# A gated linear recurrence followed by an MLP mixer: one batch's v loaded in fp32, and some transposes moved to the DMA crossbar

## The chip, the cores and the metric

The kernel runs on one core of one Trainium2 chip. The core has five engines that work side by side, each through its own list of instructions in order: PE (TensorE, the matrix multiplier), DVE (VectorE), ACT (ScalarE), POOL (GpSimd) and SP (SyncE, which here only starts transfers). Sixteen DMA engines move data between memory and the chip's buffers; SP and POOL each feed them through a queue of their own. The metric is the device time of one execution in microseconds (us); lower is better. Before the change the median of three runs is 182.91 us (181.78 to 183.03).

## The reference

The input is `q`, `k`, `v` and `alpha`, each of shape (batch 4, heads 8, sequence 768, head size 48), and four weight matrices. All of it is fp32.

```python
for t in range(S):                               # S = 768, per batch and head
    state = alpha[t][:, None] * state + outer(k[t], v[t])   # 48 x 48
    y[t] = q[t] @ state
x  = y with the heads side by side               # (4, 768, 384)
h  = relu(x.T @ w_tok1) @ w_tok2                 # mixes along the sequence, 768 -> 256 -> 768
u  = x + h.T
out = u + relu(u @ w_ch1) @ w_ch2                # mixes along the channels, 384 -> 1536 -> 384
```

## The kernel before

**Attention in chunks.** The recurrence is computed in chunks of 128 steps, six per batch, numbered n = 0 to 23 over all batches (batch 3 is n = 18 to 23). In a chunk, ACT takes the logarithm of alpha (`ln`, line 412), PE sums it along the steps (`cum`, line 418), and ACT exponentiates it with both signs (`ea`, `ei`). POOL multiplies k (`kk`, line 434), and POOL or DVE multiplies q (`qq`, line 438), into bf16. PE then transposes both with eight 128x128 transposes into PSUM (`trk`, `trq`, line 454), and ACT or DVE copies the result to the buffer `tp` (line 458). From `tp` PE computes the 128x128 scores (`gt`, line 469), DVE masks them (`mask`, line 472), and PE multiplies them with v and adds the carried state (`y`, lines 507 and 511). `st`, `sa` and `ss` update the state. The result `x` is copied out of PSUM.

**Batch 0 in pairs.** Batch 0 is handled by `attention_pair`: two neighbouring chunks of four heads each, with rows taken two at a time, so that one run in memory is 384 bytes long (two rows of 48 fp32 numbers). Its alpha, k and q come through SP's queue in loads of four heads (`load_pair`, line 744). Its v comes through POOL's queue in six transfers that turn fp32 into bf16 on the way (`load_vz`, line 723) and write into the places between zeros of a buffer `vz`: rows 0 to 63 hold one chunk's v in the first half and zeros in the second, rows 64 to 127 the reverse. The zeros are set once (line 952). `st` and `y` (lines 634 and 666) read `vz`. All other loads (`load`, line 733) bring one chunk with all heads, in runs of 192 bytes.

**Mixer.** Per batch, `mixer` does `tok1` (line 766), `ht` (relu), `tok2` (line 788), `u` (line 798, the sum x + h), then needs u with channels on the partitions. For the first half of batch 0 that is computed directly (`tt`, lines 812 and 817). For every other half PE transposes u in nine 128x128 transposes (`utp`, line 834), in parts of six and three, and DVE or ACT copies them to `ut` (line 840). Then follow `ch1` (line 853), `rt` (relu, lines 860 and 861), `ch2` (line 875), the last sum `o` (line 881) and the store `out` (line 884) on SP's queue. `wload` (line 400) brings the weights through POOL's queue, in eight transfers that also turn fp32 into bf16: `wt1`, `wt2`, three of `wc1` and three of `wc2`.

**The order.** All operations form a graph with dependencies and buffers. `schedule` is a list scheduler that runs when the program is built: with assumed durations it takes, of the operations that could start about now, the one with the lowest number in `RANKS` (a list of names; loads of batch 0 have their own list `LOADS`), and also chooses between engines and buffers. `NOT_BEFORE` gives a few operations an earliest planned time, and `SW` is a fixed list of the stretches in which POOL's transfers are assumed to slow SP's. The result is only an order: on the chip every engine works through its list and waits for its inputs, not for planned times. `fill` puts 70 multiplications without use (`warm_`, line 377) into the list for PE where nothing else is ready; 18 more (`warm`, line 366) start the program. The first fill begins after 5 us of planned time.

Of the kernel before, what the change touches and what calls it, by code (L numbers as in the profile page):

```python
# [9 lines left out]
BF16 = mybir.dt.bfloat16  # L10
AF = mybir.ActivationFunctionType
ALU = mybir.AluOpType
# [28 lines left out]
ch2_3_5b_1 trk6 vb18 utp2_0_0 out1_0 mask17 ss9 cum17 u1_4 ch1_1_1_11 rt3_1_10 ch2_2_5_1 ei14 ch2_2_4_2 tok2_2_3
gt13 out0_1 kk21 cum9 vb9 ch1_0_0_6 ut3_0_1 y10 u3_1 trq15 tok1_0_1_0 utp3_1_0 tok1_2_0_3 rt0_0_5 gt2 gt23 kk2 o0_3
tok1_1_0_3 rt0_1_8 ch2_3_3_1 ea6 tok1_1_1_0 rt1_1_8 trk12 ea17 rt2_0_8 ch1_3_0_4 trk19 ei11 lvz1 ch1_3_1_10 ut1_0_1
ut0_0_2 mask0 trk1 trq6 rt2_1_4 st9 ut2_0_0 gt6 st6 cum23 ea13 ch1_0_0_4 rt0_0_1 ut0_1_0 rt1_1_1 gt1 ch2_0_2_0
utp3_1_1 ch1_3_0_10 rt1_0_7 ch1_0_0_5 gt4 ch2_0_5_1 y17 ss14 ch1_2_0_5 rt2_1_3 trq20 u1_1 ch2_3_2_1 trq12 ea21
tok1_1_0_5 tok2_0_4 ea23 tk5 vb23 ch1_2_1_11 ch1_3_0_7 u3_0 u3_2 ch2_3_1_1 u0_2 ss12 ei8 kk3 st12 mask5 ht2_1 aq11
kk17 trk18 aq5 mask14 ln15 tp9 ht0_0 ch2_2_2_1 sa20 ln7 gt22 ch1_3_1_9 tok2_1_0 tok1_1_1_3 ln12 o2_2 rt3_0_11 tk0
ss1b ei9 st16 rt0_1_5 u2_5 u0_1 y2 o3_5b qq4 rt3_0_6 ch2_2_3_1 o2_1 ei18 trk4 aq0 trk21 ut0_0_1 ss2 tp7 ln19 ln5 y1
cum7 cum2 y0 gt16 ea4 tok1_0_1_5 y21 vb12 ln2 ea19 o3_4 ea8 rt1_0_5 ch1_3_0_6 ch1_0_0_0 ei5 ch1_2_0_10 st15 rt0_0_3
rt2_1_7 aq7 vb19 out3_0 rt3_0_2 ut1_1_1 sa7 ut3_1_0 rt3_1_5 out2_4 ei7 tok2_3_4 mask10 ei13 tt0_1 trk9 ei2 ln21  # L50
ch2_2_2_2 mask7 trq23 utp1_0_0 ch1_1_1_10 rt0_1_10 ei23 ea11 ch1_3_1_7 ch1_1_1_5 o3_3 lvz2 cum15 out3_2 rt1_1_10
ch1_0_1_7 sa22 st21 out1_5 trk8 ss7 ch2_3_2_0 ch1_0_0_1 kk6 qq5 tp18 x7 ss3 gt15 cum8 tp16 trq22 kk0 aq23 ss1 qq23
ln4 wwt1 u1_0 st18 st20 x10 utp0_1_0 qq14 ch2_1_2_0 ch1_3_0_0 out0_3 rt0_1_7 aq10 rt3_1_2 rt2_1_1 o3_5a trk23 ln18
x3 ut2_1_1 rt0_1_3 out3_3 trk20 gt0 st3 st7 rt3_1_9 st1 rt2_1_2 tp6 tok2_0_3 ch1_0_0_2 ut2_1_0 trk16 wwc20 rt1_1_4
ea10 rt3_0_9 ch1_0_0_3 st4 y9 tok2_0_5 rt1_1_11 wwc10 y16 trq3 ch1_0_0_11 utp0_1_1 rt3_0_1 ln1 ss6 ch1_3_1_6
ch1_3_1_2 ea3 ch1_0_0_9 rt0_1_0 trq19 trq8 ch1_1_1_0 tok1_3_0_0 u3_3 x17 aq15 tok2_0_2 qq10 x1 qq21 tok2_3_0 out3_1
ch2_1_0_2 lvz5 trq13 aq16 ch1_0_1_4 tok2_0_1 ch1_0_1_1 ch1_0_1_11 aq12 rt1_0_1 cum11 ch1_0_1_6 trq11 out1_4 tok2_3_1
tok1_3_0_3 ch1_0_0_7 ch1_2_0_7 ch1_0_1_3 o2_3 ut0_0_0 vb22 tok2_1_1 tok2_0_0 mask15 ea12 trq21 st14 u2_0 gt3
ch2_0_2_1 tok2_1_3 wwc21 ch1_0_1_5 aq3 u0_4 rt0_0_11 st22 ch1_0_1_0 vb16 trk7 tp23 wwc22 mask8 ss3b rt0_0_8 trq5
qq19 rt2_1_10 ch1_0_1_9 mask21 ss5 rt0_1_4 ei1 tok1_1_0_0 ln22 tok2_2_1 ch2_3_4_2 rt3_0_10 tk1 tok1_1_1_5 ln9 st19  # L60
out0_4 utp1_0_1 y7 ch1_0_1_10 rt0_0_6 ch2_3_5a_1 kk15 x15 kk8 rt3_0_4 ch1_0_1_8 ch2_0_0_0 aq18 utp2_0_1 rt1_0_11
out3_4 out1_1 ch2_2_4_0 ch2_3_0_0 y11 ch2_0_5_0 ea15 ch1_3_1_5 vb13 o0_4 tq3 u2_1 rt3_1_4 aq1 ch1_3_1_1 rt2_1_6
tok1_3_1_0 qq20 ch2_0_1_0 ss4 ch2_2_0_2 ch2_0_3_0 tok2_1_5 tp10 ss22 trq0 ch1_1_1_9 ch1_3_0_8 mask4 y23 u0_0
ch1_3_0_5 rt0_0_9 tok1_0_1_3 o1_2 vb21 mask6 rt0_1_9 tok1_0_0_5 ch1_2_1_2 rt2_1_0 tok2_1_4 rt3_0_8 st5 lvz0 mask3
utp3_0_1 rt1_0_9 cum22 aq8 kk13 ch2_2_1_1 ss21 ch2_3_1_0 rt1_0_2 trq10 out1_3 ln3 kk19 gt14 rt3_0_3 rt2_0_3 tok2_2_2
ch2_3_1_2 mask13 ch1_2_1_1 ut2_0_1 ch1_1_1_7 kk22 ch1_2_0_4 ln8 tq1 tok1_3_1_5 o2_4 aq17 o3_1 ch2_2_5_2 ht1_1 ei12
aq20 y22 ss15 y18 ln14 ch1_2_1_7 kk5 ch1_1_1_2 ss10 gt11 rt1_0_6 st3b ch1_2_0_2 ch2_1_3_2 st13 rt0_1_6 ss16
ch2_0_3_2 y12 rt1_1_2 out0_5 ch1_1_0_10 tq5 cum0 u2_2 tok1_2_0_5 vb20 out3_5b x22 tok2_2_0 rt2_1_5 ht1_0 ch2_3_0_1
vb6 out0_0 cum20 ch1_1_0_5 vb7 gt17 x4 rt3_1_0 ei4 rt2_0_5 o2_5 gt10 utp2_1_0 ch1_1_1_6 aq13 ei20 cum6 ch1_3_1_0
rt0_0_4 ch2_1_1_1 trk22 o0_0 ch2_3_4_1 ea7 wwc12 ch1_1_1_8 ch1_1_0_1 rt0_0_0 trk14 ei21 ln20 ch2_0_1_2 cum18 u1_2  # L70
ch1_2_1_8 ch1_2_0_3 ch1_1_0_2 ss19 ch2_1_1_0 rt2_0_7 rt3_1_6 out1_2 o3_0 out2_5 ch2_2_1_2 ch1_2_1_3 tok2_2_4 u2_3
ch1_3_0_3 qq0 tq0 rt0_1_1 cum19 rt1_0_0 ei17 ch2_3_5b_2 u0_3 x2 ln11 ch1_2_1_10 o0_5 x12 wwc11 trq18 ht3_1 rt0_0_10
qq9 rt2_0_11 ch2_3_2_2 ch1_1_0_0 vb14 ch1_1_0_3 o2_0 tok1_2_1_3 y5 st8 ei10 ss2b tp21 qq15 rt2_0_9 aq6 trk11 y15
ei22 tok1_2_1_5 aq14 ch1_2_0_8 rt0_0_2 utp2_1_1 sa14 ch2_1_2_2 trq14 ch1_3_1_3 ch1_1_0_9 x19 tok1_2_0_0 rt3_1_8 kk11
rt0_1_2 mask18 trk15 utp1_1_0 vb8 tp22 o0_1 kk1 u0_5 mask9 trk0 ch1_1_0_6 rt3_1_7 ch1_3_1_8 ch1_1_0_11 ch1_2_0_1
ch1_2_0_0 ch2_2_0_1 qq16 ss18 rt2_1_8 u3_5 ch1_3_0_1 out2_2 ut1_0_0 ea0 x13 cum14 sa21 aq2 ea9 rt0_0_7 ea5 st0
ch1_2_1_5 sa16 ch2_3_5a_2 ch2_1_5_2 st1b ch1_1_0_4 kk7 y19 out2_1 mask22 ch2_1_3_0 ln6 tp14 x14 st2b tok2_2_5 cum13
# [132 lines left out]
def schedule(ops, slots, sw=()):  # L210
# [20 lines left out]
    while ready:  # L231
# [41 lines left out]
        if o.dma:  # L273
            o.done = dmas.land(o.dma[0], t, *o.dma[1:])
# [779 lines left out]
```

## Time and profile before

| what | value |
|---|---|
| median of three runs | 182.91 us |
| the profiled execution's own time | 182.94 us |
| its span (first to last instruction) | 181.2 us |
| PE busy | 173.9 us, 96% of the span |
| ACT busy | 108.5 us, 60% |
| DVE busy | 105.4 us, 58% |
| POOL busy | 59.7 us, 33% |
| SP's queue, all loads and stores | 22.42 MB, 59.6% of 16 engines |
| POOL's queue, v of batch 0 and the weights | 3.74 MB, 14.2% of 16 engines |
| granted TensorE clock | 1.00 |

The profile is of one execution. The span leaves out 1.7 us of the execution's own time that lie around it. Busy times of PE overlap, since a multiplication begins before the one ahead of it has ended: one 128x384 multiplication is listed with 326 ns, but 36 in a row took 5.85 us. Idle time of an engine that is not the limit costs nothing. Shares over the whole span are averages over stages with different limits, and the stages are what has to be read.

### The profile page before, as it was taken

The numbers are of one execution on the slowest core, as the hardware profiler recorded it, in microseconds if no ns is written. First come the engines' busy times: TensorE is split into PE (matmuls) and PEld (weight loads), VectorE is DVE, ScalarE is ACT, GpSimd is POOL, SyncE is SP. The second block draws the span as 40 slices with busy tenths as digits, with TensorE's granted clock in tenths as the row PEclk, the third lists the DMA queues.
The fourth block names the chain that finished last, engine by engine and source line by source line (L and its number), as shares of the span: only waits on it lengthen the run. The fifth ranks groups of instructions, "written<-read, shape, count | busy, mean of one in ns | idle before, by whom it ended". The sixth has DMA issues, their size and how long they took to land.

```text
span 181.2 us, 4740 instructions
## 1 busy us (share of the span) xinstructions
PE 173.9 (96%) x1922; PEld 120.7 (67%) x1922; DVE 105.4 (58%) x190; ACT 108.5 (60%) x219; POOL 59.7 (33%) x94
## 2 busy tenths in 40 slices
PE   7897899999999999999899999999999999999994
PEld 4575788677676676677677666577666566676663
DVE  6674676694972665886975579565556652130142
ACT  3456785577894567799787675879732204948000
POOL 8922886020942336456361722403030000000000
PEclk9999999999999999999999999999999999999999
DMA  5999999998999899999999999910002121110123
GB/s 133 201 202 245 225 176 200 194 191 171 203 196 198 159 194 178 201 185 238 205 217 182 228 169 205 259 60 4 0 0 89 45 87 43 47 43 0 43 90 130
DMA packets 93861, 26.45 MB, mean 146 GB/s; under 512 B 88080, under 2 KB 93456, under 8 KB 93840
## 3 DMA queue, kind: packets, MB, share of 16 engines
q1 hardware_dynamic: 87984, 22.42, 59.6%
q0 software_dynamic: 5856, 3.74, 14.2%
q8 instruction: 15, 0.25, 0.6%
q14 instruction: 6, 0.05, 0.1%
HBM read 25.17 MB, written 4.72 MB: 165 GB/s over the span
## 4 chain that ended last, share of the span: by engine, by line
PE 64%; DMA 23%; SPq 4%; ACT 2%; DVE 2%; issue 1%; POOL 1%; DVEq 0%; POOLq 0%; ACTq 0%
PE ps L853 21%; PE ps L875 19%; DMA at_pair<-in_alpha_dram 15%; SPq L744 4%; PE ps L766 3%; PE ps L788 3%; DMA vt_pair<-in_v_dram 3%; PE ps L454 3%; DMA qt_pair<-in_q_dram 3%; DMA at<-in_alpha_dram 3%; PE ps L377 2%; PE p L469 2%; PE ps L834 1%; PE ps L507 1%; PE ps L666 1%
## 5 line engine op out<-in xcount | busy, mean ns | idle before, releaser
L853 PE MATMUL ps<-ut,wc 128*128 128x384 bf16 x288 | 54.3, 326 | 0.9 <-DVE ut L840 0.5
L875 PE MATMUL ps<-wc,rt 128*128 128x384 bf16 (+1 forms) x300 | 52.7, 319 | 0.0
L860 ACT ACTIVATE rt<-ps 128x384 bf16<-128x384 f32 x85 | 41.8, 494 | 12.9 <-PE ps L853 12.4
L853 PEld LDWEIGHTS <-wc 128*128 128x128 bf16 x288 | 30.7, 114 | 13.3 <-issue 1.7
L875 PEld LDWEIGHTS <-rt 128*128 128x128 bf16 x300 | 27.8, 98 | 15.5
L881 DVE TENSOR_TENSOR o<-ps,u 128x384 f32<-128x384 f32 (+1 forms) x25 | 13.3, 540 | 21.6 <-PE ps L875 21.2
L472 DVE TENSOR_TENSOR gtm<-p,u 128x1024 bf16<-128x1024 f32 x18 | 22.0, 1220 | 6.8 <-PE p L469 6.8
L434 POOL TENSOR_TENSOR pkk<-kt_pair,ia 128x384 bf16<-128x384 f32 x15 | 15.3, 1017 | 24.3 <-ACT ia L428 24.2
L798 DVE TENSOR_TENSOR u<-ps,x 128x384 bf16<-128x384 f32 x24 | 12.7, 550 | 6.7 <-PE ps L788 6.7
L458 ACT COPY tp<-ps 128x1024 bf16<-128x1024 bf16 x13 | 13.2, 1014 | 3.3 <-PE ps L454 3.3
L377 PE MATMUL ps<-warm_in 128*128 128x256 bf16 x70 | 13.9, 290 | 0.0
L445 POOL TENSOR_TENSOR acq<-a,bm 128x8 f32<-128x8 f32 x18 | 5.7, 317 | 24.0 <-ACT a L426 22.5
L412 ACT ACTIVATE la<-at_pair 128x384 bf16<-128x384 f32 x15 | 7.9, 528 | 8.7 <-DMA at_pair<-in_alpha_dram 8.6
L788 PE MATMUL ps<-ht,wt 128*128 128x384 bf16 x48 | 11.0, 326 | 0.0
L438 DVE TENSOR_TENSOR pkq<-qt_pair,a 128x384 bf16<-128x384 f32 x9 | 7.1, 784 | 6.1 <-DMA qt_pair<-in_q_dram 4.4
L492 DVE TENSOR_TENSOR sum<-ps,ss 128x384 f32<-128x384 f32 x12 | 6.6, 552 | 6.2 <-PE ps L483 6.2
L766 PE MATMUL ps<-x,wt 128*128 128x384 bf16 x48 | 9.9, 326 | 0.0
L428 ACT ACTIVATE ia<-ps 128x384 f32<-128x384 f32 x18 | 8.9, 492 | 1.3 <-PE ps L421 1.3
L840 ACT COPY ut<-ps 128x384 bf16<-128x384 bf16 (+1 forms) x7 | 4.2, 611 | 9.0 <-PE ps L834 9.0
L426 ACT ACTIVATE a<-ps 128x388 f32<-128x388 f32 x18 | 8.8, 491 | 0.6 <-PE ps L421 0.5
L515 ACT CAST x<-ps 128x384 bf16<-128x384 f32 x12 | 5.8, 481 | 5.1 <-PE ps L511 5.0
L611 DVE TENSOR_TENSOR gtm<-p,mask_pair 128x1024 bf16<-128x1024 f32 x6 | 7.3, 1223 | 2.0 <-PE p L606 1.8
(118 smaller groups left out, 267.1 us busy)
## 6 DMA issues: line engine op xcount, KB each, us to landing
out_dram<-o SPq DMA_DIRECT2D x23, 192.0 KB, 3.0
at_pair<-in_alpha_dram SPq DMA_DIRECT2D x21, 192.0 KB, 4.5
kt_pair<-in_k_dram SPq DMA_DIRECT2D x21, 192.0 KB, 4.7
qt_pair<-in_q_dram SPq DMA_DIRECT2D x21, 192.0 KB, 4.8
vt_pair<-in_v_dram SPq DMA_DIRECT2D x14, 192.0 KB, 4.4
wc<-in_moe_w_ch_dram POOLq DMA_DIRECT2D x6, 384.0 KB, 9.1
vt<-in_v_dram SPq DMA_DIRECT2D x4, 192.0 KB, 4.0
wt<-in_moe_w_tok_dram POOLq DMA_DIRECT2D x2, 384.0 KB, 7.1
```

Source lines behind the costliest of these rows:

```text
L377: last = g.op("PE", f"warm_{i}", lambda e, ps=ps: e.matmul(ps()[:, 0:256], lhsT=E.warm_in[:, 0:128], rhs=E.warm_in, start=True, stop=True, ...
L428: g.op("ACT", f"ei{n}", lambda e: e.activation(ia(), cum()[:, 0:HD], AF.Exp, scale=-1.0), act_us(384), reads=[cum], writes=[ia])
L434: g.op("POOL", f"kk{n}", lambda e: e.tensor_tensor(pkk()[:, :, 0:D], T["kt"](), hd(ia()), ALU.mult), (1.03, 1.0), reads=[T["kt"], ia], wri ...
L458: lambda e: (e.copy if e is E.act else e.tensor_copy)(tp(), ptp().bitcast(BF16).rearrange("p (j t) -> p j t", t=128)),
L472: g.op("DVE", f"mask{n}", lambda e: e.tensor_tensor(gtm(), E.p23.rearrange("p (j t) -> p j t", t=128), E.mask8, ALU.mult), (1.24, 1.22), r ...
L766: e.matmul(ps()[:, 0:HD], lhsT=E.b_wt1[:, kc, m * 128:m * 128 + 128], rhs=x[kc](), start=(kc == 0), stop=(kc == NS - 1), skip_group_check= ...
L788: e.matmul(ps()[:, 0:HD], lhsT=E.b_wt2[:, kc, i * 128:i * 128 + 128], rhs=ht[kc](), start=(kc == 0 and not summed), stop=(kc == NDT - 1))
L798: g.op("DVE", f"u{b}_{i}", lambda e, ps=ps, t=t, i=i: e.tensor_tensor(t(), ps()[:, 0:HD], x[i](), ALU.add), dve_us(384), reads=[ps, xt[i]] ...
L853: e.matmul(ps()[:, 0:384], lhsT=E.by_four[mc // 4][:, kc, mc % 4, :], rhs=uts[half]()[:, kc * 384:kc * 384 + 384], start=(kc == 0), stop=( ...
L860: e.activation(rtt[mc]()[:, cs], ps()[:, 0:384], AF.Relu) if e is E.act else
L875: e.matmul(ps()[:, 0:n], lhsT=rtt[mc]()[:, i * 128:i * 128 + 128], rhs=E.b_wc2[:, mc, cs], start=(mc == 0), stop=(mc == NDC - 1), skip_gro ...
L881: g.op("DVE", f"o{tag}", lambda e, ps=ps, t=t, i=i, cs=cs, n=n: e.tensor_tensor(t()[:, cs], ps()[:, 0:n], u[i]()[:, cs], ALU.add), dve_us( ...
```

## The change

1. **v of batch 0.** `load_vz` is gone. v is now loaded like q, in fp32 by SP's queue (`ldvt`), and 12 new operations `vc` cast it into the six buffers `b_vz` beside the zeros, 64 partitions by 384 elements each, on ACT, DVE or POOL.
2. **Loads of batch 0.** Only the first pair of chunks is still loaded in two groups of four heads. The other two pairs are loaded with all eight heads at once. There are 16 loads in place of 18 and six transfers on POOL's queue. The list `LOADS` begins with v.
3. **k with q of batch 3.** For n = 18 to 23 k and q are written into one buffer (`s_pk`), and one DMA on SP's queue, `dtk`, transposes it through the crossbar into `tp`. `trk`, `trq` and the copy `tp` are gone there.
4. **u of batches 2 and 3.** Three tiles of u share one buffer (`s_u3`), and one DMA on SP's queue per half, `dtu`, transposes it into `ut`. `utp` and the copies `ut` are gone there. `ch1` reads the new layout through `channels`.
5. **Buffers and planner.** `rt` has 18 buffers and, from batch 1 on, the six `vz` buffers too (before 24); `u` has 12 (13), `o` 6 (7), `pkk` 4 (6), `acq` 5 (6). In the planner SP waits when over 2048 runs are in flight, and a transpose holds SP until the transfers ahead of it are done. `RANKS`, `LOADS`, `NOT_BEFORE` and `SW` are new throughout.

```diff
-LOADS = {n: i - 2999.0 for i, n in enumerate("""ldat0 ldkt0 ldat2 ldqt0 ldkt2 ldat4 ldqt2 ldat1 ldqt1 ldat3 ldat5 ldqt4 ldkt1 ldkt3 ldqt3 ldkt4 ldkt5 ldqt5""".split())}
-NOT_BEFORE = {"lvz0": 3.0, "lvz1": 3.6432229280593225, "lvz2": 3.5646344861793087, "lvz3": 3.0, "lvz4": 3.0,
-              "lvz5": 6.784296118108255, "wwt1": 18.201532689715037, "wwt2": 20.604694224156404, "wwc10":
-              23.228101551750406, "wwc11": 33.44407754651961, "wwc12": 26.882706927650386, "wwc20":
+LOADS = {n: i - 2999.0 for i, n in enumerate("""ldvt0 ldat1 ldvt1 ldvt2 ldat0 ldkt0 ldkt1 ldat2 ldqt1 ldqt0 ldkt2 ldqt2 ldkt4 ldat4 ldqt4 ldvt4""".split())}
+NOT_BEFORE = {"wwt1": 15.268526730144032, "wwt2": 17.868047160368754, "wwc10": 37.09580914814636, "wwc11":
+              3.784711466738922, "wwc12": 28.05532928830701, "wwc20": 46.56128458051416, "wwc21":
...
+            if e == "SP":
+                turned = dmas.hw_end - o.dma[1] if o.dma[3] == 129 else 0.0
+                free[e] = max(free[e], dmas.gate(), turned)
...
+    SPLIT = (0,)
+    CROSS_KQ, CROSS_U = tuple(range(18, 24)), (2, 3)
...
+        if crossbar:
+            g.op("SP", f"dtk{n}", lambda e: e.dma_start_transpose(
+                tp(), tk().rearrange("p w h d -> p (w h d)")), (1.3, 1.3), reads=[tk], writes=[tp],
+                dma=("hw", 0.9, 1.0, 129))
+        else:
+            g.op("PE", f"trk{n}", lambda e: f_tr(e, 1, pkk), (0.225, 0.225 + DRAIN), reads=[tk], writes=[ptp])
+            g.op("PE", f"trq{n}", lambda e: f_tr(e, 0, pkq), (0.225, 0.225 + DRAIN), reads=[tq], writes=[ptp])
...
-        vz = T["vz"]
+        vz = g.tile(self.s_vz[ci])
+        for hh in range(2):
+            g.op(("ACT", "DVE", "POOL"), f"vc{n}_{hh}", lambda e, r=slice(64 * hh, 64 * hh + 64), hh=hh: (
+                e.copy if e is E.act else e.tensor_copy)(E.b_vz[ci][r, hh], of("vt")[r]),
+                [(0.39, 0.49), (0.36, 0.35), (0.53, 0.5)], reads=[T["vt"][grp]], writes=[vz], joint=True, lock=True)
...
-            g.op("POOL", f"lvz{n + hh}", lambda e, hh=hh, ts=ts: e.dma_start(
-                t()[64 * hh:64 * hh + 64, hh, :, :],
-                E.d_v[b, :, ts:ts + 128, :].rearrange("h (p c) d -> p h (c d)", c=2)),
-                (0.68, 0.68), writes=[t], joint=True, at=6.0 + 3.0 * ci + 0.1 * hh, dma=("sw", 1.6, 0.37))
...
+            if b in self.CROSS_U:
+                g.op("SP", f"dtu{b}_{half}", lambda e, t=t, h=ut3[3 * half]: e.dma_start_transpose(
+                    t().rearrange("p (j t) -> p j t", t=128), h()), (1.35, 1.35), reads=[ut3[3 * half]],
+                    writes=[t], dma=("hw", 1.0, 1.0, 129))
+                uts.append(t)
+                continue
...
+        def channels(t, kc):
+            if b in self.CROSS_U:
+                return t.rearrange("p (i j t) -> p j i t", i=3, j=3)[:, kc]
+            return t[:, kc * 384:kc * 384 + 384]
```

More of the change, by code (lines that the diff above doesn't have):

```diff
@@ L74 @@
[L74 to L77, printed above, removed]
-ln16 o1_5 o1_1 trq4 ei15 out3_5a y20 ch2_1_5_0 ch1_3_1_11 ch2_2_3_0 o0_2 ch1_1_0_8 ch2_2_4_1 mask20 ch2_2_5_0 aq4
@@ L206, in land @@
         self.hw_end = t + left
+        self.flying.append((t + left, runs))
         return t + left + 1.2
```

249 lines of the change are left out of this document (136 added, 113 removed), and 4 rows, old and new, of the table PLAN.

## The prediction

> **What bounds the kernel now.** I read the page first: the span, the busy engines, the slices, the chain.
>
> ```profile
> span 181.2 us, 4740 instructions
> PE 173.9 (96%) x1922; PEld 120.7 (67%) x1922; DVE 105.4 (58%) x190; ACT 108.5 (60%) x219; POOL 59.7 (33%) x94
> ...
> DMA  5999999998999899999999999910002121110123
> ...
> PE 64%; DMA 23%; SPq 4%; ACT 2%; DVE 2%; issue 1%; POOL 1%; DVEq 0%; POOLq 0%; ACTq 0%
> ```
>
> PE is busy nearly throughout. The DMA engines are as full up to slice 26 (about 118 us), and the chain gives them 23%. So the question is which of the two sets the end, and the stages answer it:
>
> ```profile
> 120.00:140.00 20.00, 20.00 (x238) 13.83 (x237) 11.48 (x17) 12.58 (x26) 3.01 (x4) 1.00 0.07 24
> 140.00:160.00 20.00, 20.00 (x146) 13.02 (x143) 7.88 (x15) 7.31 (x15) 0.00 (x0) 1.00 0.14 51
> ```
>
> ```profile
> 30.60:177.80 147.20, 146.08 (x1553) 99.61 (x1551) 84.76 (x134) 90.48 (x184) 38.95 (x57) 1.00 0.68 136
> ```
>
> The columns are the stretch, its length, the busy time of PE, PE's weight loads, DVE, ACT and POOL, then PE's clock, the DMA share and GB/s. From 30.6 to 177.8 us PE idles 147.20 - 146.08 = 1.1 us, at clock 1.00. A busy PE need not be one at its rate, so I look at the chain in order of time:
>
> ```profile
> 41.21 0.45 PE ps L454 x8
> ...
> 120.91 0.44 PE ps L834 x6
> ...
> 160.40 5.85 PE ps L853 x36
> 166.25 11.73 PE ps L875 x84
> ```
>
> 36 multiplications of 384 columns in 5.85 us are 0.1625 us each, packed without a gap. The 23% of DMA in the chain is how the walk back passes through loads in the middle; PE did not stop for them there. So **PE's work from 30.6 us on sets the end**: what leaves PE there comes off the time, and what delays the start of that stretch is added.
>
> What sets 30.6? The last logarithm of batch 0, and the first multiplications of the mixer:
>
> ```profile
> 17.20 0.52 ACT L533 ACTIVATE la<-at_pair 128x384 bf16<-128x384 f32 x1 [0.81 <-DMA at_pair<-in_alpha_dram]
> ```
>
> ```profile
> 30.59 1.14 PE L766 MATMUL ps<-x,wt 128*128 128x384 bf16 x6
> ```
>
> ```profile
> 17.00:30.60 13.60, 12.41 (x225) 10.27 (x223) 9.44 (x16) 9.75 (x19) 10.13 (x14) 1.00 1.09 203
> ```
>
> Batch 0's last alpha is there at 17.2 us, and 13.4 us of work on POOL (10.13 busy), ACT (9.75) and DVE (9.44) in turns follow. Up to 30.6 us PE partly does fill. The head is thus bound by batch 0's loads and then by that chain.
>
> **The change part by part.**
>
> *Transposes off PE.* Batch 3: six chunks of eight, 48. Batches 2 and 3: four halves of nine, 36.
>
> ```profile
> L454 PE MATMUL ps<-id,pkk 128*128 128x128 bf16 x72 | 7.0, 219 | 0.0
> L454 PE MATMUL ps<-id,pkq 128*128 128x128 bf16 x72 | 7.0, 219 | 0.0
> ...
> L834 PE MATMUL ps<-id,u 128*128 128x128 bf16 x63 | 5.7, 219 | 0.0
> ```
>
> The 219 ns overlap; in the chain eight take 0.45 us and six 0.44 us, or 0.056 us each (0.073 in the short piece, with its run-in). I take 0.056: 84 x 0.056 = **4.7 us** off PE. Batch 3's first transposes stand here:
>
> ```profile
> 100.57 0.39 PE L454 MATMUL ps<-id,pkk 128*128 128x128 bf16 x4
> ```
>
> So all of it comes off after 100 us, where PE is full. The copies out of PSUM go too (six `tp`, eight parts of `ut`):
>
> ```profile
> L458 ACT COPY tp<-ps 128x1024 bf16<-128x1024 bf16 x13 | 13.2, 1014 | 3.3 <-PE ps L454 3.3
> ```
>
> They lie on ACT and DVE beside a full PE (12.58 and 11.48 of 20 us), so they are worth nothing by themselves. The new access of `ch1` reads the same 384 columns in three pieces of 128, in 144 multiplications. At the rate of 128-column ones (3 x 0.056 = 0.169 against 0.1625 us) that would be 0.9 us, at best 0; I take 0, since it stays one instruction.
>
> *Crossbar transposes.* The trace has none, so I bound one by other transfers. SP's queue late in the kernel holds stores alone, and the landing times are min, median and max:
>
> ```profile
> 113.52 65.22 SPq L884 DMA_DIRECT2D out_dram<-o  x20
> ```
>
> ```profile
> DMA to landing us min/median/max: 1.6/1.9/5.1
> ```
>
> ```profile
> kt_pair<-in_k_dram SPq DMA_DIRECT2D x21, 192.0 KB, 4.7
> ```
>
> Low end 1.9 us (a quiet queue), high end 4.7 us (among loads). The path replaced is 0.45 + 1.01 = 1.5 us. So a result comes 0.4 to 3.2 us later than PE's, ten times. What hides that is PE's other work; today's order leaves this between transposes and scores:
>
> ```profile
> 128.60 0.39 PE L454 MATMUL ps<-id,pkq 128*128 128x128 bf16 x4
> 128.83 1.63 PE L853 MATMUL ps<-ut,wc 128*128 128x384 bf16 x9
> 130.38 0.42 PE L469 MATMUL p<-tp 48*64 48x128 bf16 x16
> ```
>
> That is 1.8 us filled with `ch1`. The new planner assumes 1.0 + 0.9 + 1.2 = 3.1 us from issue to landing, and its order will put about that much `ch1` and `ch2` in between; 120 to 160 us hold enough of it. The first ones, from 100.6 us on, meet a full DMA queue, those after 113.5 us a quiet one. I take 0.3 us lost in all; the bounds are 0 and, with no cover, 32 us. Behind a waiting `dtk` or `dtu` on SP stand later loads and stores. Loads run far ahead (the last issue is before 113.5 us, and the scores at 130.38 still work on what they brought), so a few us of lateness there cost nothing; a store costs only at the end, where no transpose is left.
>
> *v by SP's queue, in fp32.* POOL's six issues go, 3.65 us of five of them ahead of the first `kk`:
>
> ```profile
> 3.02 3.65 POOL L723 DMA_DIRECT2D vz<-in_v_dram  x5
> ```
>
> The bytes read stay. The packet counts of 2 to 6, 8 to 14 and 2 to 21 us:
>
> ```profile
> q1 hardware_dynamic: 2483, 0.93, 95.7%
> ```
>
> ```profile
> DMA packets 4372, 1.22 MB, mean 204 GB/s; under 512 B 4372, under 2 KB 4372, under 8 KB 4372
> ```
>
> ```profile
> q1 hardware_dynamic: 10201, 3.66, 85.3%
> q0 software_dynamic: 3168, 0.59, 36.7%
> ```
>
> SP's queue alone made 2483 / 4 = 621 packets per us; both queues together 4372 / 6 = 729. Batch 0 has four inputs of 768 x 384 fp32 in runs of 384 bytes, 3072 x 4 = 12288 packets. Today they are through at about 20 us (13369 by 21 us, the last of them batch 1's); by one queue from 2 us on, 12288 / 621 = 19.8 us bring it to 21.8: up to **1.8 us later**. The Trainium skill ("DMA: Bandwidth & Descriptors", Issuing engines are not separate DMA queues) says that transfers of all queues run on the same 16 engines and that spreading them only saves issue time; by that rule this term would be 0 and the head's upper bound lower by it. The rows, 621 against 729, speak against the rule here.
>
> *Weights in the head.* `wc11` may now start at 3.8 us of planned time, when POOL has nothing else, so it goes first on POOL. The size of such a transfer, and what one does to SP's queue, at 32 to 38 us and, without one, at 40 to 44:
>
> ```profile
> wc<-in_moe_w_ch_dram POOLq DMA_DIRECT2D x6, 384.0 KB, 9.1
> ```
>
> ```profile
> q0 software_dynamic: 929, 0.92, 90.2%
> q1 hardware_dynamic: 1178, 0.22, 30.6%
> ```
>
> ```profile
> q1 hardware_dynamic: 3451, 0.65, 83.5%
> ```
>
> SP's rate falls from 863 to 196 packets per us, by 77%, and 384 KB (0.39 MB) of weights at 0.92 / 6 = 0.153 MB per us last 2.6 us: 2.0 us of delay for the loads of the head. `wt1` starts earlier too and may meet the last loads.
>
> *Against that:* k of both chunks of a pair now arrives ahead of the next pair (today `kt1`, `kt3` and `kt5` come late), POOL is lighter by 3.65 x 6 / 5 = 4.4 us, and only v, needed last in a chunk, ends late. Alpha of the last pair ends at packet 10240 of 12288: 2 + 10240 / 621 = 18.5 us, 20.5 with `wc11`, where today it is 17.2. From there only the last two chunks remain.
>
> *Casts.* Twelve `vc` on half the partitions; the same free size costs
>
> ```profile
> L440 ACT CAST vb<-vt_pair 128x384 bf16<-128x384 f32 x6 | 3.1, 519 | 0.3 <-DMA vt_pair<-in_v_dram 0.2
> ```
>
> 0.52 us each, 6.2 us over three engines in 25 us, of which at most the last one (0.5) is on the path. The zeros are as many bytes as before; fewer buffers could stall, but each batch needs 12 `rt`, and 24 remain after batch 0. For the head I sum bounds: later data +3.8, casts +0.5, against the 3.65 us of issues that stand ahead of POOL's first `kk` today and may come off in full. I take **0**, near the middle of -3.65 to +4.3.
>
> *The refitted orders* touch every engine's list. With 1.1 us idle from 30.6 on there is next to nothing left to win; a bad order could lose, which I leave to the range.
>
> **Sum**, against the profiled execution's own 182.94 us (its span and 1.7 us around it; the median of the runs is 182.91): -4.7 + 0.3 + 0 = -4.4, **178.5 us**.
>
> **Rivals.**
>
> *The head gets shorter.* POOL's first `kk` no longer waits for 3.65 us of issues, and k comes in time. Against it: the two-queue rate. At -2.5 us: 176.0.
>
> *The head gets longer.* One queue and `wc11` cost the full 3.8 us and nothing is won back; PE's work is still 4.4 us less: 178.5 + 3.8 = 182.3, within 1%. For it: the rates above; against: 13.4 us pass today between the last alpha and 30.6, so data isn't all.
>
> *The crossbar is late, and the kernel slower.* Place: scores of chunks 18 to 23 and `ch1` of four halves. A transpose that waits for the transfers ahead and lands after 4.7 us plus 1.3 us of issue takes 6.0 where the order has 3.1: 2.9 us each where PE, which keeps its order, comes to the scores first. Two exposed ones (5.8 us) eat the gain; from three on (8.7) the kernel is slower by over 1%: 178.5 + 3 x 2.9 = 187.2. For it: the full queue before 113 us. Against: PE's slip at the first one gives the later ones room, and the later ones come after 113.5 us.
>
> *The crossbar works block by block.* Eight or nine blocks of 128x128 in turn, each with a small store's least landing time, 1.6 us, would hold SP's queue for 6 x 12.8 + 4 x 14.4 = 134 us; from 100.6 us on, with `ch1` and `ch2` of the last half (5.85 + 11.73 us) behind them, the end would be near 252. The Trainium skill ("VectorE: DVE Perf Modes", The three transpose paths) advises TensorE where PSUM will do, and gives 1309 ns for one 128x128 block by the crossbar against 390 on TensorE; estimated by that page, block by block, the queue would be held for 110 us. No run here shows it yet, and transfers of 192 KB landing in 1.9 us are a sign against such slow pieces.
>
> **How the numbers follow.** Forecast 0.46 (own range 177 to 181), shorter head 0.11, longer head 0.18, late crossbar 0.20, block by block 0.05. A measurement of this kernel tells some 1% from no change: faster means below 181.1, slower above 184.7. Faster 0.46 + 0.11 = 0.57; same 0.18; slower 0.25. For 8 in 10 the range leaves out the last case and most of the late crossbar: 175.8 to 186.0.
>
> **What would show it.** Right: no L454 rows for batch 3, L834 with 27 transposes in place of 63, PE idle after the head still some 1 to 2 us, the first mixer row (L766) within 3 us of 30.6. Wrong: PE waits on a DMA at the scores or at `ch1` after 95 us (crossbar), the first L766 past 34 us (head), or waits on SP's queue that reach PE. A transpose's issue and landing will be in the DMA rows.

## The result and the profile after

The changed kernel takes 185.14 us (median of four runs, 184.81 to 185.68) against 182.91 us before; the ratio, from runs on one chip, is 1.014 with an interval of 1.009 to 1.019. A second measurement of the same kernel, shown below, gave 1.010 (1.005 to 1.016). **It is slower, by about 1%.** The prediction said 178.5 us, faster, with 175.8 to 186.0 as its range. Ratios here and below leave out runs more than 1.5% above the fastest of the same kernel, which matters most for `e_u3`, where three of six are left out.

The page of the changed kernel, with the lines that answer to those quoted of before:

```profile
span 183.1 us, 4587 instructions
PE 169.2 (92%) x1838; PEld 117.6 (64%) x1838; DVE 98.3 (54%) x182; ACT 108.0 (59%) x227; POOL 57.4 (31%) x89
...
DMA  5999999999999998999999899999530053320113
...
PE 70%; DMA 16%; ACT 6%; SPq 4%; DVE 2%; issue 1%; POOL 1%; ACTq 0%
```

PE has the 84 multiplications less that the change takes away (1922 to 1838) and 4.7 us less busy time (173.9 to 169.2), as forecast. Its share of the span fell, though, from 96% to 92%: the work went and idle time came. DMA stays full longer, up to slice 28 in place of 26.

The idle time shows in the timeline of PE at the end of the head (first the kernel before, then the changed one), and in the stretch from there to PE's end (columns: stretch, length, busy time of PE, its weight loads, DVE, ACT, POOL, then clock, DMA share, GB/s):

```profile
31.79 1.14 PE L766 MATMUL ps<-x,wt 128*128 128x384 bf16 x6
```

```profile
34.62 1.38 PE L788 MATMUL ps<-x,wt 128*128 128x384 bf16 x6
```

```profile
34.60:179.40 144.80, 140.86 (x1466) 95.22 (x1465) 77.29 (x122) 87.47 (x186) 38.24 (x54) 1.00 0.80 152
```

The last `tok1` group of batch 0, which in the same view of the kernel before starts at 31.79 us, starts at 34.62: the head is 2.83 us longer. (The prediction took an earlier group of the first view, at 30.59, as the head's end; here last is compared with last.) Behind it PE idles 144.80 - 140.86 = 3.94 us, where it idled 1.1: another 2.8. So +2.8 + 2.8 - 4.7 = +0.9; the last fill of PE starts 1.46 us later than before, and 0.5 us are left unassigned. These sizes are of one execution each. In the profile of the second measurement PE's waits behind the head come to 5.1 us, and the same head code ended between 31.12 and 33.40 us in two profiles of one kernel (`e_u3` in the table below).

PE's waits behind the head (engine, line, released by; us in total, times, longest):

```profile
PE ps L894 <- DMA ut<-u: 1.6, 1, 1.6
PE ps L788 <- ACT x L547: 1.0, 1, 1.0
PE ps L397 <- ACT ut L876: 0.4, 1, 0.4
PE ps L817 <- DVE o L922: 0.4, 1, 0.4
PE p L501 <- DMA tp<-pk: 0.2, 1, 0.2
```

One `ch1` waits for a transposed half of u, one `tok1` for an x from ACT; a transposed chunk of k and q is late by 0.2 us once. Why x is late shows in ACT's waits from 60 to 125 us:

```profile
ACT vb L467 <- DMA vt_pair<-in_v_dram: 7.3, 4, 4.3
ACT la L432 <- DMA at_pair<-in_alpha_dram: 4.6, 5, 2.5
```

ACT works in order, and waits 11.9 us for loads of v and alpha, which then holds up all that stands behind on it. Before the change ACT, DVE and POOL together waited longer for loads in this stretch, 28.9 us against 15.7, but for v mostly on POOL. The rows of the casts of v with the longest waits, before and after:

```profile
L440 POOL CAST vb<-vt_pair 128x384 bf16<-128x384 f32 x4 | 2.0, 505 | 10.0 <-DMA vt_pair<-in_v_dram 10.0
```

```profile
L467 ACT CAST vb<-vt_pair 128x384 bf16<-128x384 f32 x8 | 4.1, 516 | 7.4 <-DMA vt_pair<-in_v_dram 7.3
```

The refitted order has two of these 18 casts on POOL, where the old one had six; what it would bring to put them back was not tried. The transposes stand on SP between these loads. Their rows on SP's timeline (start, time that they held SP):

```profile
98.53 3.07 SPq L483 DMA_TRANSPOSE tp<-pk  x1
110.71 1.94 SPq L483 DMA_TRANSPOSE tp<-pk  x1
113.92 1.37 SPq L483 DMA_TRANSPOSE tp<-pk  x1
...
116.62 1.18 SPq L753 DMA_DIRECT2D vt_pair<-in_v_dram  x1
```

Three of them hold SP for 6.4 us ahead of the last load, which is issued at 116.62 us; before the change it was issued at 112.53:

```profile
112.53 0.94 SPq L733 DMA_DIRECT2D vt_pair<-in_v_dram  x1
```

The two kernels' lists differ there in more than the transposes, so this is not yet their price. From issue to landing (min, median, max) a transpose of k and q takes 3.1/4.0/4.9 us, one of u 3.3/3.6/5.0:

```profile
DMA to landing us min/median/max: 3.1/4.0/4.9
```

### The profile page after: what moved, and what is told of

It reads as the page before. It is cut to its first block, busy times and chain, and to the rows that moved or that the text cites. A ratio compares the mean times of both kernels' runs of the same rounds, so it can differ in the third digit from the quotient of the medians.

```text
span 183.1 us, 4587 instructions
## 1 busy us (share of the span) xinstructions
PE 169.2 (92%) x1838; PEld 117.6 (64%) x1838; DVE 98.3 (54%) x182; ACT 108.0 (59%) x227; POOL 57.4 (31%) x89
## 4 chain that ended last, share of the span: by engine, by line
PE 70%; DMA 16%; ACT 6%; SPq 4%; DVE 2%; issue 1%; POOL 1%; ACTq 0%
PE ps L894 23%; PE ps L916 20%; DMA at_pair<-in_alpha_dram 5%; DMA kt_pair<-in_k_dram 4%; PE ps L788 4%; DMA tp<-pk 4%; PE ps L817 3%; DMA ut<-u 3%; PE ps L481 3%; PE p L501 3%; PE ps L397 2%; SPq L753 2%; SPq L765 2%; PE ps L539 2%; PE ps L617 1%; PE ps L438 1%
## 5 line engine op out<-in xcount | busy, mean ns | idle before, releaser
L916 PE MATMUL ps<-wc,rt 128*128 128x384 bf16 (+1 forms) x222 | 44.6, 322 | 0.0
L901 ACT ACTIVATE rt<-ps 128x384 bf16<-128x384 f32 x66 | 31.8, 492 | 19.5 <-PE ps L894 19.3
L916 PEld LDWEIGHTS <-rt 128*128 128x128 bf16 x222 | 21.0, 98 | 12.2
L504 DVE TENSOR_TENSOR gtm<-p,u 128x1024 bf16<-128x1024 f32 x18 | 21.9, 1219 | 10.1 <-PE p L501 9.9
L916 PE MATMUL ps<-wc,vz 128*128 128x384 bf16 (+1 forms) x78 | 19.1, 314 | 0.0
L461 POOL TENSOR_TENSOR pkk<-kt_pair,ia 128x384 bf16<-128x384 f32 x10 | 10.0, 997 | 21.0 <-ACT ia L448 18.4
L490 ACT COPY tp<-ps 128x1024 bf16<-128x1024 bf16 x8 | 8.1, 1012 | 4.7 <-issue 2.4
L901 ACT ACTIVATE vz<-ps 128x384 bf16<-128x384 f32 x20 | 9.8, 490 | 1.0 <-PE ps L894 1.0
L916 PEld LDWEIGHTS <-vz 128*128 128x128 bf16 x78 | 7.5, 98 | 4.0
L547 ACT CAST x<-ps 128x384 bf16<-128x384 f32 x17 | 8.1, 478 | 2.7 <-PE ps L543 2.2
L461 POOL TENSOR_TENSOR pk<-kt_pair,ia 128x384 bf16<-128x384 f32 x5 | 5.5, 1108 | 13.0 <-ACT ia L448 12.6
```

The lines of the kernel that those rows point to most:

```text
L461: g.op("POOL", f"kk{n}", lambda e: e.tensor_tensor(pkk()[:, :, 0:D], T["kt"](), hd(ia()), ALU.mult), (1.03, 1.0), reads=[T["kt"], ia], wri ...
L504: g.op("DVE", f"mask{n}", lambda e: e.tensor_tensor(gtm(), E.p23.rearrange("p (j t) -> p j t", t=128), E.mask8, ALU.mult), (1.24, 1.22), r ...
L901: e.activation(rtt[mc]()[:, cs], ps()[:, 0:384], AF.Relu) if e is E.act else
L916: e.matmul(ps()[:, 0:n], lhsT=rtt[mc]()[:, i * 128:i * 128 + 128], rhs=E.b_wc2[:, mc, cs], start=(mc == 0), stop=(mc == NDC - 1), skip_gro ...
```

## The experiments

All kernels keep the planner's list and edit it afterwards, so that only the named operations change place; each engine's other work keeps its order. `move(name, behind, engine)` puts an operation behind another, and on another engine if one is given. Ratios are to the kernel before, run on the same chip; its median was 182.9 to 184.4 us, depending on the chip, and ratios are to be compared, not times. The last column is of one profiled execution each.

| kernel | ratio | interval | last `tok1` group of batch 0, us |
|---|---|---|---|
| changed kernel | 1.014, again 1.010 | 1.009 to 1.019, 1.005 to 1.016 | 34.62, 34.73 |
| a_wc11: one weight later | 1.013 | 1.007 to 1.019 | 30.99 |
| a_casts: last casts to POOL | 1.011 | 1.001 to 1.021 | 36.17 |
| a_loads: alpha and k first | 1.013 | 1.006 to 1.020 | 34.96 |
| a_head: all three | 1.013 | 1.004 to 1.022 | 35.03 |
| b_wc2: a_wc11, wc2 apart | 1.008 | 1.004 to 1.012 | 31.73 |
| r_kq: k, q back on PE | 1.006 | 1.002 to 1.009 | 33.65 |
| r_u: u back on PE | 1.012 | 1.007 to 1.016 | 33.68 |
| r_both: both back on PE | 1.021 | 1.017 to 1.025 | 33.70 |
| b_kq: b_wc2 and r_kq | 1.012 | 1.006 to 1.017 | 36.80 |
| a_no_v: no v of batches 1 to 3 | 0.972 | 0.967 to 0.978 | 33.03 |
| b_no_v: b_wc2 without that v | 0.964 | 0.956 to 0.973 | 30.79 |
| r_both_no_v: r_both without it | 1.003 | 1.000 to 1.007 | 34.76 |
| before_no_v: before without it | 0.987 | 0.980 to 0.994 | 33.08 |
| e_u3: before, three halves of u by crossbar | 0.988, again 1.002 | 0.981 to 0.995, 0.998 to 1.006 | 31.12, 33.40 |

### The head

**a_wc11**

```diff
+ move("wwc11", "wwt2")            # on POOL; it was POOL's first work
```

> One edit of the changed kernel: the second third of wc1 is issued by POOL behind wt2, not as POOL's first work. Theory A (the head is longer because k waits behind other data): that weight's packets took the place of some 1,200 packets of SP's queue between 6 and 10 us, 1.7 us at the 700 per us of the free stretches; the first kk goes from 11.63 to about 10 us, the last group of tok1 of batch 0 from 34.62 to about 33.2, and the time from 185.1 to about 183.5. Theory B (the head ends late because of ACT's casts of v and its order near 24 to 28 us): the first kk starts earlier, but the last group of tok1 stays within 0.4 us of 34.6 and the time within 0.5 us of 185.1.

The packets of SP's queue (q1) from 6 to 10 us, in the changed kernel and in this one:

```profile
q0 software_dynamic: 400, 0.39, 64.5%
q1 hardware_dynamic: 1448, 0.54, 53.5%
```

```profile
q1 hardware_dynamic: 2837, 1.06, 118.3%
```

1389 packets more pass, 2.0 us at this queue's 2837 / 4 = 709 per us. The first `kk` and the last `tok1` group move as theory A said, and further:

```profile
9.80 0.99 POOL L596 TENSOR_TENSOR pkk<-kt_pair,ia 128x384 bf16<-128x384 f32 x1 [1.25 <-DMA kt_pair<-in_k_dram]
```

```profile
30.99 1.38 PE L788 MATMUL ps<-x,wt 128*128 128x384 bf16 x6
```

The head is 3.6 us shorter than the changed kernel's and 0.8 us shorter than that of before. So v in fp32 by one queue, with its casts, costs the head nothing that shows here; the whole of its lengthening goes with that one weight. Yet the time hardly moves. The rows of SP, DVE and PE around 50 us, where the gain went:

```profile
46.63 4.58 SPq L753 DMA_DIRECT2D qt_pair<-in_q_dram  x1
...
54.66 0.36 DVE L467 CAST vb<-vt_pair 128x384 bf16<-128x384 f32 x1 [5.75 <-DMA vt_pair<-in_v_dram]
...
55.54 1.12 PE L894 MATMUL ps<-ut,wc 128*128 128x384 bf16 x3 [5.16 <-DVE rt L902]
```

PE came to this point 3.6 us earlier; v of chunk 9 did not. DVE stood 5.75 us for it, with a relu behind it that PE needed for a free bank.

**a_casts, a_loads, a_head**

```diff
+ move("vc4_1", "aq2", "POOL"); move("vc4_0", "aq2", "POOL"); move("vc5_1", "kk5", "POOL")
```

```diff
- ldvt0 ldat1 ldvt1 ldvt2 ldat0 ldkt0 ldkt1 ldat2 ldqt1 ldqt0 ldkt2 ldqt2
+ ldat1 ldkt1 ldat0 ldkt0 ldvt1 ldvt0 ldat2 ldqt1 ldqt0 ldkt2 ldvt2 ldqt2
```

> One edit of the changed kernel: the three casts of v of the last pair that ACT runs at 25.73 to 27.33 go to POOL, two ahead of qq of that pair, one behind its second kk. Theory B (casts on ACT's chain): ia of chunk 5 moves from 27.33 to about 26.6, where the cum that it reads ends, and everything behind it by 0.7 us; last group of tok1 about 33.9, time about 184.4. Theory A (only the first k counts): the chain moves but what follows is held by the other chunks, tok1 stays within 0.3 us of 34.6 and the time at 185.1.

> One edit of the changed kernel: on SP's queue alpha and k of the first pair come first, then v of the first pair, then the rest; the casts of pairs 0 and 1 stand later, on DVE and ACT. The queue's bytes are the same, and the last pair's loads keep their places. Theory A: the first kk moves from 11.63 to about 7 us (6.74 before the change), the last group of tok1 from 34.62 to about 32, and the time to about 182.5. Theory C (one queue that carries v too is the bound, by the last pair's data near 22.3 us): the first kk moves as much, but the last group of tok1 stays within 0.5 us of 34.6 and the time at 185.

> The three edits together (weight later, last casts off ACT, alpha and k first). Theory A with B: the head is as long as before the change or shorter, last group of tok1 at 31.0 to 32.0 us, time 181.5 to 182.5, so that only what PE loses behind the head is left against the 178.5 forecast. Theory C: the last pair's data still come at 20.6 us or later, last group of tok1 at 33 or later, time 183.5 or more.

a_casts and a_loads both miss theories A and B. In a_loads the first `kk` starts 5 us earlier, and the last `tok1` group no earlier:

```profile
6.45 0.98 POOL L596 TENSOR_TENSOR pkk<-kt_pair,ia 128x384 bf16<-128x384 f32 x1
```

```profile
34.96 1.37 PE L788 MATMUL ps<-x,wt 128*128 128x384 bf16 x6
```

That is theory C: the head's end hangs on what the queue brings last, not on its first k. The trace adds a place that theory C did not name. The last two chunks run 1.2 us ahead of the changed kernel's (their last score products but one at 28.68 us), until ACT stands 1.66 us, up to 30.16, for batch 1's first alpha, which landed 10.1 us after its issue. The casts on POOL made things worse, by an edit of mine; in a_head POOL stands 2.92 us at v of the last pair, ahead of q and k that were there:

```profile
23.09 1.25 POOL L590 CAST vz<-vt_pair 64x384 bf16<-64x384 f32 x2 [2.92 <-DMA vt_pair<-in_v_dram]
```

ACT there also stands 1.14 us for batch 1's first alpha. So a_head says nothing of the three causes' sum, and theory B is not borne out.

### What takes the gain back

**b_wc2**

```diff
+ move("wwc11", "wwt2")
+ move("wwc20", "aq8"); move("wwc21", "qq9"); move("wwc22", "wwc21")
```

> The kernel with the later second third of wc1, and beside it wc2's three loads apart: the first (the one that the first matmuls of the channel mixer's second product read) where all three stood, the other two one chunk later on POOL. Theory D (the 3.6 us that the head gained were given back where three wc2 loads in a row kept SP's queue still, so that v of chunk 9 came 5.75 us late for DVE): that wait falls from 5.75 to under 2 us, PE's 5.2 us of idle there to under 1.5, and the time is 180.5 to 183. Theory E (the stretch from 20 to 60 us is bound by the sum of the transfers, wherever they stand): PE's idle only moves to another place before 65 us, 3 us or more in all, and the time stays above 184.

Here and below, the timeline's stretch of 36.60 to 116.60 us (behind the head, with loads) is read with PE's columns alone: length, busy time, clock, DMA share, GB/s. First the kernel before, then the changed one, then b_wc2:

```profile
36.60:116.60 80.00, 78.88 (x961) 1.00 1.05 197
```

```profile
36.60:116.60 80.00, 77.97 (x939) 1.00 1.09 192
```

```profile
36.60:116.60 80.00, 75.37 (x911) 1.00 1.09 191
```

The 5.2 us wait is gone, in its place stand two of 3.0 us in all, and others later: the idle time in this stretch is 4.63 us against the changed kernel's 2.03 (3.21 in its repetition). The head gained 2.9 us, the idle time took 2.6 back here, or 1.4 by the repetition. That is theory E. The DMA share is above 1 in all three.

**r_kq, r_u, r_both**: transposes back on PE, with the rest of the change in place.

```diff
- SP: dtk18 .. dtk23                        # r_kq, r_both
+ PE: 8 transposes of pk(n) into PSUM bank 1;  ACT or DVE: tp(n) <- bank
- SP: dtu2_0 dtu2_1 dtu3_0 dtu3_1           # r_u, r_both
+ PE: 6 and 3 transposes of u3 into a bank;  ACT or DVE: ut <- bank
```

> The changed kernel with k and q of batch 3 transposed on PE again: eight transposes for each of chunks 18 to 23 into the bank that batches 1 and 2 use, one copy for each on ACT (four) or DVE (two); SP's six transposes gone, u still by crossbar. Theory P (the transposes by crossbar pay, but less than their PE time, because of waits): PE gets 48 x 0.056 = 2.7 us more and loses about 1.2 us of waits (x late behind ACT's waits for loads 1.0, tp 0.2), time 186.5. Theory Q (their hold on SP's queue costs as much as they save): time 185.1 or less. Theory N (they cost nothing): time 187.8.

> The changed kernel with u of batches 2 and 3 transposed on PE again: nine transposes and two copies for each of the four halves; k and q of batch 3 still by crossbar. Theory P: PE gets 36 x 0.056 = 2.0 us more and loses the 1.6 us that it waited for ut near 124 us, time about 185.5. Theory Q: the freed queue also brings loads earlier, time 184.5 or less. Theory N: time 187.1.

> Both together: no transpose by crossbar is left, PE has its 84 transposes again, the head and the refitted order of all else stay. Theory P: PE's waits behind the head fall from 3.9 to about 1.1 us (as before the change) while its work grows by 4.7 us, time about 187.0; then before the change and this kernel differ by the head and the order alone. Theory R (the waits behind the head come from the refitted order and from fewer buffers): they stay at 3 us or more, time 188.5 or more.

r_kq gives PE 48 transposes back and is not slower: 1.006 against 1.014 and 1.010 (its interval overlaps that of the second). That is theory Q. The waits for ut and for x are gone from PE's list, and the last load is issued earlier:

```profile
PE ps L817 <- DVE o L922: 0.9, 1, 0.9
PE ps L894 <- ACT vz L901: 0.7, 1, 0.7
PE ps L397 <- ACT ut L876: 0.5, 1, 0.5
```

```profile
113.29 0.70 SPq L753 DMA_DIRECT2D vt_pair<-in_v_dram  x1
```

u by crossbar, on the other hand, saves something once k and q are off SP: from r_kq to r_both the ratio goes from 1.006 to 1.021, apart by far more than the intervals, 2.8 us for 2.0 us of transposes. With `dtk` in the queue too (the changed kernel against r_u) it saves nothing that can be told. r_both lands on theory P's 187: all transposes off PE together save 0.7 to 1.1%, 1.3 to 2.0 us, of the 4.7. But its idle time behind the head did not fall to before's 1.1 us, as P said: up to 165 us it is 3.5 us, which is what theory R (order and buffers) expected of it, though not of the time. Where PE idles tells the two causes apart:

| PE's idle time, us | 36.6 to 80 | 80 to 98.5 | 98.5 to 125 |
|---|---|---|---|
| kernel before | 0.37 | 0.52 | 0.23 |
| changed kernel, again | 0.00, 0.00 | 0.57, 1.95 | 3.29, 2.18 |
| r_both | 0.43 | 2.78 | 0.20 |

The changed kernel's first `dtk` is issued at 98.53 us. Behind that point its idle time is 2 to 3 us above r_both's, so this part goes with the transposes. r_both's own idle time lies ahead of it, so the transposes can't be its cause. In r_both DVE alone waits this for v from 60 to 105 us, before any `dtk` of the changed kernel:

```profile
DVE vb L467 <- DMA vt_pair<-in_v_dram: 6.2, 4, 2.4
```

This pointed away from the crossbar and to the loads.

**after_2, a_no_v, b_no_v**: the changed kernel again, and two kernels without the 18 loads of v of batches 1 to 3.

```diff
- SP: ldvt6 .. ldvt23
```

> The changed kernel as it is, for comparison with the three beside it on one chip: 1.009 to 1.019 of the time of the kernel before, last group of tok1 of batch 0 near 34.6 us (33.7 in the kernels with k and q or u on PE), PE's waits behind the head 3.5 to 4.5 us.

> The changed kernel without the 18 loads of v of batches 1 to 3 (each chunk casts what its buffer holds from batch 0): one load in four is gone from SP's queue behind the head, all else stands. Theory L (behind the head the loads set the pace, and SP's holds for the transposes hurt through them): PE's idle in 35 to 180 us falls from 3.9 to 2 us or less, the 1.0 for x at 107 us goes, the 1.6 for ut at 124 us shrinks since the queue runs ahead, time 182 to 183.5. Theory X (the crossbar's own landing time makes the waits): the idle stays above 3 us, the time at 184.5 to 185.5.

> The same without those 18 loads in the kernel with the second third of wc1 later and wc2 apart, whose head ended 2.9 us earlier but whose time gained only about 0.5%. Theory L: the gain of the head now stays, PE's idle in 35 to 180 us is at most 2.5 us (6.4 with the loads), time 179 to 181.5. Theory X: the idle stays at 4.5 us or more, time 183 or more.

The repetition missed its expectation in the waits, 5.1 us against 3.5 to 4.5. Theory L holds, and the effect is more than twice what I expected: 0.972 against 1.010, some 7 us. The two stretches of a_no_v, with loads and without (116.60 to 165.00 us):

```profile
36.60:116.60 80.00, 79.61 (x986) 1.00 0.95 167
116.60:165.00 48.40, 48.32 (x389) 1.00 0.35 82
```

The same of the changed kernel on this chip:

```profile
36.60:116.60 80.00, 76.79 (x931) 1.00 1.05 187
116.60:165.00 48.40, 46.31 (x412) 1.00 0.57 120
```

Idle time 0.47 us in place of 5.30, the head 1.7 us shorter (the first load of chunk 6's v stood within it, and PE's clock from 12 to 20 us was 0.85 in place of 0.58; their shares are open), and 1.1 of the 7.6 us by which PE's last fill is earlier left unassigned. The transposes by crossbar are all there, and neither ut nor tp is waited for; so their landing time by itself costs nothing here. ACT's waits for alpha are gone as well, though no alpha load was taken out. Without v the shorter head of b_no_v seems to last: 0.964, though its interval overlaps a_no_v's.

**r_both_no_v, before_no_v**: the same loads left out of the kernel with all transposes on PE, and of the kernel before.

```diff
- SP: ldvt6 .. ldvt23                       # both
+ POOL: v's buffers <- 0, behind wwc11      # before_no_v
```

> The changed kernel with all 84 transposes on PE and without the same 18 loads of v; to be compared with the changed kernel without them (ratio 0.972, 179.0 us). Theory L: where the loads do not pace it, the transposes by crossbar save all of their PE time, so this kernel is 4 to 4.7 us slower than that one, ratio 0.995 to 1.000. If the transposes by crossbar have a cost of their own beside the loads: less than 3 us between the two, ratio under 0.99.

> The kernel before the change without the loads of v of batches 1 to 3 (the buffers are set to zero once on POOL, in its idle time near 32 us, and the casts read them). Theory L (the loads pace what is behind the head, and the kernel before has PE work just long enough to cover them): PE's waits behind the head, 1.1 us, fall to 0.5 or less, the head by at most 1 us, the time by 1 to 2 us, ratio 0.990 to 0.995. If the kernel before is paced by the loads as much as the changed one, the ratio is near 0.97.

r_both_no_v against a_no_v is what the crossbar saves where loads do not set the pace: 1.003 - 0.972 = 3.1%, 5.7 us; 1.7 of the 6.8 us between their last fills stand in the head, which neither edit touches, so about 5.1 are left, against 4.7 forecast. And the kernel before gains only 1.3% (2.4 us, a little more than the 1 to 2 expected) where the changed one gains 4%: its PE idles 0.13 us in this stretch without the loads and 1.12 with them.

```profile
36.60:116.60 80.00, 79.87 (x981) 1.00 0.82 158
```

So PE and loads ran nearly level before the change. r_both is the closer control, since it has the changed kernel's order and the old PE work: without these loads it goes from 1.021 to 1.003, or 1.8%, and its idle time in this stretch from 3.21 to 0.39 us. So its waits were waits for loads too, which the refitted order lets through to PE. The step from 1.8% to 4% goes with the transposes. It is shown that the loads take back most of what they save; how much of that is PE's smaller work, which covers the loads less, and how much the transposes' own place in SP's queue, these runs do not separate.

### Two attempts at something faster

**b_kq** joins the edits of b_wc2 and r_kq.

> Weights as in the kernel with wc2 apart, k and q of batch 3 back on PE, u of batches 2 and 3 still by crossbar: what the runs so far speak for. If the two gains add up (0.6% for the weights, 0.8% for k and q): the ratio to the kernel before is 0.995 to 1.002, time 182 to 183.5. Theory L (loads set the pace wherever PE gets ahead): less than the sum, 1.001 to 1.006.

It missed: 1.012, no better than either. Its profiled execution, at 185.95 us the longest of ten, idles only 1.35 us in the stretch with loads, but its head ends at 36.80 us. ACT stood 3.02 us for batch 1's first alpha, which landed 12.6 us after its issue, where it took 5.4 us in b_wc2, whose head has the same code; PE waited for ACT in turn, and its clock was 0.74 from 24 to 36 us:

```profile
30.15 0.48 PE L438 MATMUL ps<-la,u 128*128 128x384 bf16 x1 [2.38 <-ACT la L432]
```


```profile
24.00:36.00 12.00, 8.99 (x120) 0.74 1.11 192
```

A head that ends late seems to let the loads get ahead, by single profiles: the last fill starts at 179.27, 181.12, 178.97, 179.44 and 180.87 us in the changed kernel, its repetition, r_kq, b_wc2 and b_kq, with heads that end from 31.7 to 36.8.

**e_u3, e_u3_2** are the kernel before with u of three halves by crossbar, all issued behind the last load.

```diff
- PE: utp2_1, utp3_0, utp3_1; ACT, DVE: ut of them
+ SP: dtu2_1 behind u2_5, dtu3_0 behind u3_2, dtu3_1 behind u3_5
+ move("tok2_3_2", "tok2_3_1"); move("tok2_3_5", "ch1_3_0_4")   # with their sums
```

> The kernel before the change, its list kept, with u of three halves (second of batch 2, both of batch 3) by crossbar, all issued after the last load; u lies in buffers that only batch 0 used, two tok2 blocks and their sums stand some 1 to 4 us earlier. Theory L (behind the last load nothing paces PE): 27 x 0.056 = 1.5 us less, ratio 0.990 to 0.994. If a landing comes late at one of the halves (3.3 to 5.0 us from issue): a wait of 1 us or more, ratio 0.996 to 1.002.

> The kernel with u of three halves by crossbar once more, since its profiled execution was one with PE at a clock of 0.91 between 100 and 120 us and waits of 2.5 us at wc and o that no edit of it touches. Theory L: without those, PE waits for no ut at all, PE's idle in 35 to 180 us is at most 1.5 us beside its last 2 us, the ratio 0.988 to 0.996. Otherwise a wait for ut stands at one of the three halves, ratio 0.998 or more.

0.988 and 1.002: the two do not agree, and no gain is shown. In the second, undisturbed profile PE never waits for ut. It waits 1.60 us at 109.20, ahead of all these edits' transposes, behind a DVE that waited for v:

```profile
107.05 0.36 DVE L441 CAST vb<-vt_pair 128x384 bf16<-128x384 f32 x1 [2.96 <-DMA vt_pair<-in_v_dram]
...
109.20 0.95 PE L789 MATMUL ps<-ht,wt 128*128 128x384 bf16 x4 [1.60 <-DVE o L887]
```

Whether the 1.5 us of PE work come off when this wait is not there stays open. No kernel here beats the one before beyond doubt.

## Why the prediction was wrong

**Transposes off PE, -4.7: right.** 84 multiplications and 4.7 us of busy time went. Between kernels without v's loads it is worth about 5.1 us.

Of the 6.3 us between the forecast -4.4 and the profiled executions' +1.9, the head makes 2.8, PE's waits 2.5, and 1.0 is unassigned.

**"Loads run far ahead ... a few us of lateness there cost nothing": this is the step that failed.** It took the last issue at 113 us and scores at 130 us as distance. The loads were not ahead: 18 chunks of 4 loads of 1024 packets (192 KB in runs of 192 bytes) are 73,728 packets, which at the prediction's own 863 per us without a weight beside them need 85 us. The first ones went near 20 us, and the last was issued at 112.53; the weights and stores in between take what is left of these 93 us, so SP's queue had next to no time to spare. "PE's work from 30.6 us on sets the end" was true only because PE's work just covered the loads. Once PE gets ahead, by a shorter head or by the 4.7 us of work less, it meets the loads and waits, in the changed kernel between 80 and 125 us; a_no_v, without a quarter of the loads, idles 0.4 us there.

**Crossbar, +0.3: too small, and at another place.** The waits at PE grew by 2.8 us. Only 1.6 + 0.2 of them are the lateness at `ch1` and scores that the sum and the third rival had in mind; the landing times (3.1 to 5.0 us) fit the bounds. The rest comes through the loads, which ACT and DVE wait for in order, so that x is late. A transpose holds SP's queue up to 3.07 us, and with k and q back on PE the last load is issued 3.3 us earlier; that this hold is the cause, and not the smaller PE work or the casts' place, is argued. I had named the loads queued behind `dtk`, and put no price on them.

**Head, 0: the bounds held (-3.65 to +4.3), the middle did not.** It became +2.8. The term "2.0 us of delay" for `wc11` was right as a term (1389 packets, 2.0 us) and is nearly all of it; what was set against it, 3.65 us of POOL's issues, does not come off: the first `kk` starts at 11.63 us, where it was 6.74, and it is not what the head's end waits for (a_loads). A further 1.0 us is PE's clock, below. Later data by one queue, +1.8, is not seen: with the weight moved the head is 0.8 us shorter than before. The 621 packets per us behind that term were counted from 2 to 6 us; in a_wc11 SP's queue alone made 709 from 6 to 10.

**Casts, copies, `ch1`'s access, zeros at 0:** nothing in the runs speaks against it.

**Refitted orders, about 0:** too low. r_both differs from the kernel before by head, order and buffers, and is 2.1% slower, 3.9 us, of which the head is 1.9; the remaining 2 us are idle time at waits for loads. Which edit of the order brings them was not tried; the casts of v that moved from POOL to ACT and DVE are a candidate.

**Rivals.** "The head gets longer" came true in size (2.8 of its 3.8), and "late crossbar" in sign and in part of its place. By the sum each alone would have left the kernel faster by about 2 us. But the terms do not add: a_wc11 has no longer head, and is 1.3% slower all the same. "Block by block" is refuted: a transpose of eight blocks holds SP for 1.23 us at the least, and lands in 3.1 to 4.9. The Trainium skill ("VectorE: DVE Perf Modes", The three transpose paths) gives 1309 ns for one 128x128 block; here that is about the hold of a whole transfer of eight.

The best test of the prediction's foundation could have been made on paper: divide the packets that are left by the free rate of the queue, and lay the result beside PE's work.

## What to carry to other kernels

A resource at 96% of the span is not the bound alone when another is full over the same stretch: before taking work off one, compute how long the other needs for what it still has to do, by its own count and rate. A gain ahead of such a stretch (here a shorter head) is given back in it, and a loss there is partly forgiven. A transfer put into the queue that paces a kernel can cost what it holds up behind it, so count it against that queue, not only against the engine that it relieves.

## What had not been expected of the hardware

**A weight's transfer in POOL's queue halved SP's rate**: 1448 packets in 4 us beside 384 KB of `wc11`, 2837 without it. With three thirds of `wc2` in a row, two issues of SP were held for 4.58 and 3.47 us.

**A transpose held SP longest among loads**: 3.07 and 1.94 us for the first two, 1.23 to 1.66 us for the other eight, one of which (1.37) stands just ahead of the last loads. Plain loads are held too, up to 5.21 us in the same kernel.

**PE's clock in the head.** A wait of 3.91 us, until 10.82 us, has a clock of 0.59 from 12 to 20 us behind it; r_kq, whose head is the same code but waited only 1.81 us there, ran that stretch at 1.00, and its head ended 1.0 us earlier.

```profile
10.82 0.32 PE L573 MATMUL ps<-la,ub 128*128 128x384 bf16 x1 [3.91 <-ACT la L565]
```

```profile
12.00:20.00 8.00, 7.32 (x72) 0.59 1.26 262
```

```profile
12.00:20.00 8.00, 7.25 (x83) 1.00 1.27 262
```

The Trainium skill ("TensorE: Matmul & The Clock Gate", HAM oscillation — how this bites in real kernels) warns of PE idle gaps over some 3.4 us. By that rule the wait costs the slow clock as well; these rows agree, and so do the 5.16 us in a_wc11, with a clock of 0.50 from 55.5 to 60.5 us behind them. But a_head and b_kq show a low clock behind gaps of at most 2.7 us, so it is not the only cause here.
